# Left sums of the first layer kept unsplit and made by VectorE, with five weight stages and an earlier store of w_in's splits

## The chip, the cores and the metric

The kernel runs on one core of one Trainium2 chip. The metric is the device time of one execution in microseconds (us). Engines are named as the profile names them: PE (TensorE matmul), PEld (its weight loads), DVE (VectorE), ACT (ScalarE), POOL (GpSimd), SP (SyncE, which issues nearly all DMAs here).

## The reference

Three stages follow each other on 2304 tokens (4 batches of 576) of width 512.

```python
scores = scale * (q @ k.T)                     # 8 heads of 64
x = ((scores * Dmat) @ v)                      # Dmat: gamma ** (i - j), causal
h = x @ w_in;  x = relu(h) ** 2 @ w_out        # d_ff 2048
h = x @ w_in2; out = (h * clip(h + 3, 0, 6) / 6) @ w_out2
```

## The kernel before

Weights arrive as 64-bit floats and are decoded on the chip: for each piece of 128x512, `decode` gives four steps, two on ACT (`first`, L169 and L170, which read the staged words) and four instructions on DVE (`clamp` L173 and L176, `second` L182, `third` L188). A decoded fp32 tensor is then split into a high and a low fp32r part: ACT copies the high part, and the low part is a subtraction on DVE or POOL (`split_parts`, L192). Each matmul is done in three passes (high by high, high by low, low by high).

The first expert layer starts with a block of 768 tokens that runs over 16 chunks of 128 hidden units (`for c in range(NCH)`, L918). In chunk `c` PE does `h(c)` (24 matmuls, L428, in banks 6 and 7) and then `y(c-2)` (24 matmuls, L475). ACT takes `h` out of the banks (relu L444, square L447, high copy L448), so `h(c+1)` waits until the relus of chunk `c` have read them. DVE makes g's low parts (L451). Each chunk also decodes a piece A (w_out of the chunk before) and, up to chunk 13, a piece B (w_in for two chunks on), splits A (`wo`, low part on POOL) and B (`win`, low part on POOL), and stores the splits in HBM (`keep`, L406) for the blocks after it. Two `win` buffers alternate, and a staged weight is loaded into one of three buffers.

The remaining tokens run in five blocks of 768 (`BLOCKS`: two of the first layer, three of the second), 8 pairs of chunks each, with a Strassen scheme of seven products per pair (`pair`, L660; P1, P6, P2, P7, P5, P4, P3, each of 6 matmuls L675), between which the `y` steps of the pair before and side work are interleaved (`between(0)` to `between(6)`). The scheme needs four left operands per pair: w_in of two chunks (e = 0 and 1), and two sums of them, s0 and s1 (e = 2 and 3; P6 and P7 use e = 2, P5 and P3 use e = 3). `left_sums` (L500) makes the sums from decoded fp32 in four instructions of 128x256 on POOL. For the first layer this happens every second chunk, and `split_left` (L514) splits one of the two in each chunk (the tile `ready`: high on ACT, low on POOL), in chunks later than the sum; the split goes to HBM. `load_left` (L611) loads all four operands of pair k+1 from HBM at `between(0)` of pair k. The second layer's weights are decoded in time slots of seven per pair (`ready_slots`, 125 slots, in all pairs but the last of a block).

The order on each engine is that in which the code emits instructions; every engine's queue runs in order, SP's DMA issues too.

Of the kernel before, what the change touches and what calls it, by code (L numbers as in the profile page):

```python
# [74 lines left out]
def retention_moe_moe2(ctx, tc, qk, qk_last, kv, w_in, w_out, w_in2, w_out2, consts, out):  # L75

    nc = tc.nc
# [29 lines left out]
    turn = {"g": 0, "v": 0, "win": 0, "bounce": 0, "stage": 0, "decoded": 0}  # L107
# [388 lines left out]
    def store_late():  # L496
        while late_stores:
            keep(*late_stores.pop(0))

    def left_sums(a, b):  # L500
# [3 lines left out]
        op = nc.gpsimd.tensor_tensor  # L504
# [4 lines left out]
        return [a, b, s0, s1]  # L509
# [14 lines left out]
    def ready_slots():  # L524
# [16 lines left out]
        def sums(p):  # L541
            got["s", p] = left_sums(*(w32.pop((1, 2 * p + e, 0)) for e in range(2)))
# [68 lines left out]
    def load_left(k):  # L611
# [4 lines left out]
        for e in range(4):  # L616
            only = slice(1, 2) if e == 1 else slice(0, 2)
# [5 lines left out]
            lefts[j, p].append(t)  # L623

# [122 lines left out]
    halves = [(c, 0, c, 1) for c in range(1, NCH)]  # L747
# [6 lines left out]
    def next_load():  # L754

        turn["decoded"] += 1
        if coming and turn["decoded"] > 3:
            load_w(*coming.pop(0)[1:])

    with tc.manual_schedule():  # L760
# [152 lines left out]
        made = {}  # L913
# [4 lines left out]
        for c in range(NCH):  # L918
            mine, p = wins[c], c // 2
            h = emit_h(c)  # L920
            store_late()
            keep(("s", 0, p, c % 2), mine.rearrange("p a b n -> p (a b n)"), slice(c % 2, 2))
# [14 lines left out]
            for d in dec:  # L937
                for f in d:
                    f()
                next_load()  # L940
            if c >= 2:
                split_out(c - 1, nc.gpsimd)
            if c and c + 2 < NCH:
                split_in(c + 2)
            if c % 2:
                if c > 1:
                    split_left(0, p - 1, 3, made.pop(p - 1)[3])
                made[p] = left_sums(*(first_in[p][:, e] for e in range(2)))
            elif c:
                split_left(0, p - 1, 2, made[p - 1][2])  # L950
            while halves and halves[0][0] <= c:
                d = decode(*halves.pop(0)[1:])
                d.pop(0)()
                due.append(d)
# [11 lines left out]
        for d in due:  # L966
            for f in d:
                f()
            next_load()
        assert not halves  # L970
        split_out(NCH - 1, nc.gpsimd)
        pending = firsts(NCH - 2) + firsts(NCH - 1)
        store_late()
        for c in (NCH - 2, NCH - 1):
            keep(("o", 0, c), wouts[c].rearrange("p e n -> p (e n)"))
        highs[2]()
        lows[1]()
# [4 lines left out]
        lows[4]()  # L982
        load_left(1)
        uv = place("uv", [128, 4, HALF], F32, "u")
        us, vs = uv[:, :2], uv[:, 2:]
        rest = made.pop(NPAIR - 1)
        slots = [[] for _ in range(7)]
# [6 lines left out]
        for k in range(total):  # L994
# [91 lines left out]
```

## Time and profile before

| | |
|---|---|
| median of 3 runs | 875.61 us (875.46 to 879.59) |
| the profiled execution | 874.83 us |
| its span, first to last instruction | 873.0 us |
| busy: PE, PEld | 835.1 us (96%), 744.3 us |
| busy: DVE, ACT, POOL | 570.3, 457.6, 191.2 us |
| mean granted TensorE clock | 0.994 |

The span is the time between the first and the last instruction of the core; about 1.8 us of the execution lie outside it. Busy time is an average over stages; PE is busy 96% of the span, so 38 us of the span are left in which it does nothing.

### The profile page before, as it was taken

The numbers are of one execution on the slowest core, as the hardware profiler recorded it, in microseconds if no ns is written. First come the engines' busy times: TensorE is split into PE (matmuls) and PEld (weight loads), VectorE is DVE, ScalarE is ACT, GpSimd is POOL, SyncE is SP. The second block draws the span as 40 slices with busy tenths as digits, with TensorE's granted clock in tenths as the row PEclk, the third lists the DMA queues.
The fourth block names the chain that finished last, engine by engine and source line by source line (L and its number), as shares of the span: only waits on it lengthen the run. The fifth ranks groups of instructions, "written<-read, shape, count | busy, mean of one in ns | idle before, by whom it ended". The sixth has DMA issues, their size and how long they took to land.

```text
span 873.0 us, 14182 instructions
## 1 busy us (share of the span) xinstructions
PE 835.1 (96%) x5220; PEld 744.3 (85%) x5220; DVE 570.3 (65%) x954; ACT 457.6 (52%) x897; POOL 191.2 (22%) x170
## 2 busy tenths in 40 slices
PE   9989888888999999999999899999999999999997
PEld 7878777766899998899999798898898898899886
DVE  5878888888766776677666778546555446643534
ACT  1247666666756666756667654435433335433332
POOL 2354655657221330132121212100000000000000
PEclk9999999999899999999999999999999999999999
DMA  9994777797888989598987696946466453664532
GB/s 358 369 287 144 249 246 248 245 315 243 302 313 292 319 310 332 205 348 294 340 331 285 233 327 224 335 158 217 166 263 222 158 194 132 258 252 166 177 113 73
DMA packets 79115, 219.17 MB, mean 251 GB/s; under 512 B 8132, under 2 KB 24900, under 8 KB 79046
## 3 DMA queue, kind: packets, MB, share of 16 engines
q1 hardware_dynamic: 78466, 217.48, 70.8%
q8 instruction: 41, 0.67, 0.3%
q10 hardware_dynamic: 580, 0.79, 0.3%
q14 instruction: 28, 0.23, 0.1%
HBM read 167.38 MB, written 50.86 MB: 250 GB/s over the span
## 4 chain that ended last, share of the span: by engine, by line
PE 67%; DVE 13%; ACT 8%; DMA 7%; issue 3%; SPq 1%; POOL 1%; DVEq 0%; ACTq 0%; POOLq 0%
PE hps L675 30%; PE yps L635 20%; PE yps L475 10%; PE ytail L475 5%; DMA kvt<-in_kv_dram 3%; DMA stage<-in_w_in_dram 2%; DVE a L182 2%; DVE g L451 2%; DVE a L176 2%; ACT a L169 1%; ACT ready L194 1%; DVE wd L188 1%; DVE a L173 1%; DVE w L188 1%; ACT r L170 1%
## 5 line engine op out<-in xcount | busy, mean ns | idle before, releaser
L635 PE MATMUL yps<-wo,g 128*128 128x512 f32 x864 | 227.4, 394 | 3.6 <-DVE g L695 2.9
L675 PE MATMUL hps<-xlast,win 128*128 128x384 f32 x960 | 195.2, 338 | 1.3 <-DVE xlast L605 1.2
L635 PEld LDWEIGHTS yps<-wo,g 128*128 128x128 f32 x864 | 159.3, 188 | 29.2 <-DVE g L695 3.9
L675 PEld LDWEIGHTS hps<-xlast,win 128*128 128x128 f32 x960 | 167.7, 188 | 10.2 <-DVE xlast L605 1.5
L475 PE MATMUL yps<-g,wo 128*128 128x512 f32 x576 | 169.6, 400 | 3.1 <-ACT xop L600 1.4
L699 DVE TENSOR_TENSOR u<-hps,u 128x384 f32<-128x384 f32 x120 | 66.8, 557 | 159.7 <-PE hps L675 156.9
L675 PE MATMUL hps<-xop,win 128*128 128x384 f32 x720 | 147.9, 340 | 4.6 <-DVE xop L605 3.9
L675 PEld LDWEIGHTS hps<-xop,win 128*128 128x128 f32 x720 | 126.8, 190 | 12.0 <-DVE xop L605 4.3
L475 PEld LDWEIGHTS yps<-g,wo 128*128 128x128 f32 x576 | 102.0, 189 | 17.5 <-POOL wo L195 6.3
L475 PEld LDWEIGHTS ytail<-g,wo 128*128 128x128 f32 x576 | 94.4, 188 | 16.9
L693 ACT ACTIVATE g<-c 128x384 fp32r<-128x384 f32 x120 | 63.0, 525 | 84.3 <-DVE c L692 82.8
L475 PE MATMUL ytail<-g,wo 128*128 128x256 f32 x576 | 98.8, 280 | 0.0
L428 PE MATMUL hps<-xring,win 128*128 128x512 f32 (+1 forms) x384 | 72.4, 346 | 15.7 <-ACT r L444 15.7
L695 DVE TENSOR_TENSOR g<-c,g 128x384 fp32r<-128x384 f32 x120 | 70.7, 589 | 21.7 <-ACT g L693 21.4
L428 PEld LDWEIGHTS hps<-xring,win 128*128 128x128 f32 x384 | 61.1, 192 | 26.6 <-ACT r L444 18.0
L195 POOL TENSOR_TENSOR ready<-sums,ready 128x512 fp32r<-128x512 f32 x32 | 46.1, 1440 | 138.7 <-ACT ready L194 131.3
L718 ACT ACTIVATE c<-hps 128x384 f32<-128x384 f32 x40 | 19.7, 492 | 94.4 <-PE hps L675 94.4
L691 ACT ACTIVATE u<-c,three 128x384 f32<-128x384 f32 x72 | 44.4, 617 | 37.6 <-DVE c L699 36.4
L699 DVE TENSOR_TENSOR c<-hps,u 128x384 f32<-128x384 f32 x80 | 44.4, 555 | 24.4 <-PE hps L675 24.4
L182 DVE SCALAR_TENSOR_TENSOR a<-stage,a 128x512 int32<-128x512 int32 x64 | 52.1, 814 | 0.8
L692 DVE SCALAR_TENSOR_TENSOR c<-u,c 128x384 f32<-128x384 f32 x72 | 41.0, 570 | 13.4 <-ACT u L691 13.3
L173 DVE TENSOR_SCALAR a<-a 128x512 f32<-128x512 f32 x64 | 34.7, 543 | 21.3 <-ACT a L169 21.3
(95 smaller groups left out, 919.2 us busy)
## 6 DMA issues: line engine op xcount, KB each, us to landing
win<-kept SPq DMA_DIRECT2D x120, 512.0 KB
wo<-kept SPq DMA_DIRECT2D x80, 512.0 KB
kept<-ready SPq DMA_DIRECT2D x56, 512.0 KB
stage<-in_w_out_dram SPq DMA_DIRECT2D x32, 512.0 KB
win<-kept SPq DMA_DIRECT2D x40, 256.0 KB
kept<-wo SPq DMA_DIRECT2D x16, 512.0 KB
stage<-in_w_in_dram SPq DMA_DIRECT2D x16, 512.0 KB
qkt<-in_qk_dram SPq DMA_DIRECT2D x13, 512.0 KB
```

What stands on the lines that cost most here:

```text
L173: nc.vector.tensor_scalar(out=a, in0=a, scalar1=LEAST, scalar2=MOST, op0=ALU.max, op1=ALU.min)
L182: nc.vector.scalar_tensor_tensor(out=a.bitcast(I32), in0=high, scalar=-0x40000000, in1=a.bitcast(I32), op0=ALU.bitwise_and, op1=ALU.bitwis ...
L195: lambda: lo_engine.tensor_tensor(out=lo, in0=src, in1=hi.bitcast(F32), op=ALU.subtract),
L428: nc.tensor.matmul(out=h, lhsT=w[:, kk // 2, wp, kk % 2 * 128:][:, :128], rhs=xs[kk][xp][:, o:o + n], start=m == 0, stop=m == 3 * KD - 1,)
L475: nc.tensor.matmul(out=p, lhsT=w[:, wp, m * 128:m * 128 + 128], rhs=gt[:, gpart, o:o + n], start=first and e == 0 and not (k and m % 2), s ...
L635: nc.tensor.matmul(out=p, lhsT=gt[:, gpart, m * 128:m * 128 + 128], rhs=w[:, wp], start=first and e == 0, stop=last and e == 2,)
L675: nc.tensor.matmul(out=to, lhsT=wl[k][:, half if k != 1 else 0, wp, o], rhs=x[:, xp, f], start=first and m == 0, stop=last and m == 5, ski ...
L691: nc.scalar.activation(out=v, in_=c, func=ACTF.Relu, bias=three)
L692: nc.vector.scalar_tensor_tensor(out=c, in0=v, scalar=6.0, in1=c, op0=ALU.min, op1=ALU.mult)
L693: nc.scalar.activation(out=hi, in_=c, func=ACTF.Copy)
L695: lambda: nc.vector.tensor_tensor(out=lo, in0=c, in1=hi.bitcast(F32), op=ALU.subtract)
L699: nc.vector.tensor_tensor(out=out_, in0=to, in1=x, op=ALU.add)
```

## The change

It has five parts.

1. In the chunk loop the first layer's left sums are made by DVE instead of POOL, and stored as they are (fp32, one store of 512 KB per pair, key `f`) instead of as two splits (two stores of 512 KB, key `s`). The 16 `ready` splits of the first layer (ACT and POOL) go from the loop and its end.
2. For pairs of the first layer `load_left` loads the two sums unsplit (256 KB each instead of 512), and new steps `parts_of_left` split them: for pair k+1, the high part of e = 2 on ACT at `between(4)` of pair k, its low part on DVE at `between(5)`, and e = 3 one step later. For pair 0 all this is in chunk 15.
3. Five staging buffers instead of three while the first layer's weights are loaded (two more loads in chunks 2 and 3, two fewer when the second layer's loads begin).
4. The split of w_in for chunk c+1 is stored in chunk c behind the sums' store, before the store of w_out's split; the last two w_out splits are made in chunk 15 with the low part on DVE. w_out of chunk 15 is decoded together with that of chunk 14.
5. In each chunk the ACT steps of decode A come before the split of `win` and no longer after it. The second layer's slots begin seven slots sooner, as the first layer's last `split_left` steps go.

```diff
-        if turn["stage"] <= 3:
-            t = place(f"t{2 + turn['stage']}", [128, DM], mybir.dt.int64, "stage")
+        tags = ("t3", "t4", "t5") if turn["stage"] <= 3 else ("t3", "t4", None, None, None)
+        tag = None if l else tags[(turn["stage"] - 1) % len(tags) if turn["stage"] <= 3 else (turn["stage"] - 2) % 5]
...
-    def left_sums(a, b):
+    def left_sums(a, b, engine):
...
-        op = nc.gpsimd.tensor_tensor
+        op = engine.tensor_tensor
...
+            if l == 0 and e > 1:
+                t = place(f"w{4 * (k % 2) + e}", [128, 2, 2, 256], F32R, "win")
+                nc.sync.dma_start(
+                    out=t[:, 1].rearrange("p a n -> p (a n)").bitcast(F32),
+                    in_=kept["f", 0, p][:, 512 * (e - 2):512 * (e - 1)],
+                )
+                lefts[j, p].append(t.rearrange("p b a n -> p a b n"))
+                continue
...
+    def parts_of_left(k, e):
+
+        hi, lo = (lefts[divmod(k, NPAIR)][e][:, :, wp] for wp in range(2))
+        return split_parts(hi, lo, lo.bitcast(F32), nc.vector)
...
-    halves = [(c, 0, c, 1) for c in range(1, NCH)]
+    halves = [(min(c, NCH - 2), 0, c, 1) for c in range(1, NCH)]
...
-            store_late()
-            keep(("s", 0, p, c % 2), mine.rearrange("p a b n -> p (a b n)"), slice(c % 2, 2))
...
+            if c in (2, 3):
+                load()
+            store_late()
+            for n, w in ((c, mine), (c + 1, wins.get(c + 1))):
+                if w is not None and (n != c or not c):
+                    keep(("s", 0, n // 2, n % 2), w.rearrange("p a b n -> p (a b n)"), slice(n % 2, 2))
             if c >= 2:
-                split_out(c - 1, nc.gpsimd)
+                split_out(c - 1, nc.gpsimd if c < NCH - 1 else nc.vector)
+            if c == NCH - 1:
+                split_out(c, nc.vector)
+            while halves and halves[0][0] <= c:
+                due.append(decode(*halves.pop(0)[1:]))
+            for d in due[:1]:
+                d.pop(0)()
             if c and c + 2 < NCH:
                 split_in(c + 2)
             if c % 2:
-                if c > 1:
-                    split_left(0, p - 1, 3, made.pop(p - 1)[3])
-                made[p] = left_sums(*(first_in[p][:, e] for e in range(2)))
-            elif c:
-                split_left(0, p - 1, 2, made[p - 1][2])
-            while halves and halves[0][0] <= c:
-                d = decode(*halves.pop(0)[1:])
+                whole = left_sums(*(first_in[p][:, e] for e in range(2)), nc.vector)[1]
+                late_stores.append((("f", 0, p), whole.rearrange("p a n -> p (a n)")))
+            for d in due[1:]:
                 d.pop(0)()
...
+            if c == NCH - 1:
+                for e in (2, 3):
+                    parts_of_left(0, e)[0]()
+                lows[1]()
+                for e in (2, 3):
+                    parts_of_left(0, e)[1]()
...
-        slots[2].append(lambda: split_left(0, NPAIR - 1, 2, rest[2]))
-        slots[5].append(lambda: split_left(0, NPAIR - 1, 3, rest[3]))
-        slots += ready_slots()
+        slots = ready_slots()
...
+            if k + 1 < total and BLOCKS[(k + 1) // NPAIR][0] == 0:
+                for i, e in ((4, 2), (5, 3)):
+                    for n in range(2):
+                        side[i + n].append(lambda e=e, n=n: parts_of_left(k + 1, e)[n]())
```

ACT's queue in chunk 3, from the split of w_out on. `wo`, `win` and `ready` are split tiles, `a<-stage` and `r<-stage` the first steps of a decode, `r<-hps` the relu of the next chunk. Before:

```order
L194 ACTIVATE wo<-wd 128x512
L194 ACTIVATE win<-w_1334 128x2x256
L194 ACTIVATE ready<-sums 128x2x256
L169 ACTIVATE a<-stage 128x512
L170 ACTIVATE r<-stage 128x512
L169 ACTIVATE a<-stage 128x512
L170 ACTIVATE r<-stage 128x512
L444 ACTIVATE r<-hps 128x512
```

And now:

```order
L196 ACTIVATE wo<-wd 128x512
L171 ACTIVATE a<-stage 128x512
L172 ACTIVATE r<-stage 128x512
L196 ACTIVATE win<-w_1327 128x2x256
L171 ACTIVATE a<-stage 128x512
L172 ACTIVATE r<-stage 128x512
L446 ACTIVATE r<-hps 128x512
```

Decode A's steps have moved ahead of `win`, and `ready` is gone.

DVE's queue at the turn from an odd chunk to the next: the last two steps of decode B (`w_` is its output), and the first steps of decode A of the next chunk. Before:

```order
L182 SCALAR_TENSOR_TENSOR a<-stage,a 128x512
L188 ISA w_1150<-a,r 128x1024
L173 TENSOR_SCALAR a<-a 128x512
L176 TENSOR_SCALAR a<-a 128x512
L182 SCALAR_TENSOR_TENSOR a<-stage,a 128x512
L188 ISA wd<-a,r 128x1024
```

And now:

```order
L184 SCALAR_TENSOR_TENSOR a<-stage,a 128x512
L190 ISA w_1142<-a,r 128x1024
L507 TENSOR_TENSOR sums<-w_1015 128x256
L508 TENSOR_TENSOR sums<-sums,w_1015 128x256
L509 TENSOR_TENSOR sums<-w_1015 128x256
L510 TENSOR_TENSOR sums<-w_1015,sums 128x256
L175 TENSOR_SCALAR a<-a 128x512
L178 TENSOR_SCALAR a<-a 128x512
L184 SCALAR_TENSOR_TENSOR a<-stage,a 128x512
L190 ISA wd<-a,r 128x1024
```

Four instructions stand between the two decodes.

DVE's queue at the turn from chunk 15 to pair 0. `xop` and `xlast` are low parts of right operands (`lows`), `xall` a sum of operands, `u<-hps` the first use of P6's result. Before, from the last decode on:

```order
L173 TENSOR_SCALAR a<-a 128x512
L176 TENSOR_SCALAR a<-a 128x512
L182 SCALAR_TENSOR_TENSOR a<-stage,a 128x512
L188 ISA wd<-a,r 128x1024
L605 TENSOR_TENSOR xop<-t,xop 128x384 x2
L605 TENSOR_TENSOR xop<-xall,xop 128x384 x2
L605 TENSOR_TENSOR xlast<-xall,xlast 128x384 x2
L605 TENSOR_TENSOR xlast<-t,xlast 128x384 x2
L583 TENSOR_TENSOR xall<-xall,t 128x384 x2
L699 TENSOR_TENSOR u<-hps,u 128x384
```

And now:

```order
L190 ISA wd<-a,r 128x1024
L197 TENSOR_TENSOR wo<-wd,wo 128x512 x2
L507 TENSOR_TENSOR sums<-w_2119 128x256
L508 TENSOR_TENSOR sums<-sums,w_2119 128x256
L509 TENSOR_TENSOR sums<-w_2119 128x256
L510 TENSOR_TENSOR sums<-w_2119,sums 128x256
L607 TENSOR_TENSOR xop<-t,xop 128x384 x2
L197 TENSOR_TENSOR win<-win 128x512 x2
L607 TENSOR_TENSOR xop<-xall,xop 128x384 x2
L607 TENSOR_TENSOR xlast<-xall,xlast 128x384 x2
L607 TENSOR_TENSOR xlast<-t,xlast 128x384 x2
L585 TENSOR_TENSOR xall<-xall,t 128x384 x2
```

The lows of the last two w_out splits, the last sums and the lows of pair 0's left operands have come into this queue.

## Rows read from the trace of the kernel before

**Rows 1.** Busy time by stretch: us, PE, PEld, VectorE, ScalarE, GpSimd (instructions), clock, DMA, GB/s

```profile
...
80.27:88.68 8.41, 8.41 (x50) 7.32 (x49) 6.44 (x9) 4.51 (x10) 4.52 (x4) 1.00 0.57 176
...
109.22:129.76 20.54, 17.80 (x97) 14.69 (x97) 16.34 (x21) 13.54 (x27) 12.56 (x10) 1.00 0.75 243
...
211.29:234.86 23.57, 18.99 (x92) 16.64 (x91) 19.04 (x31) 15.62 (x33) 10.29 (x9) 0.86 0.82 288
234.86:480.00 245.14, 243.04 (x1377) 224.85 (x1376) 166.37 (x290) 158.09 (x315) 52.10 (x49) 1.00 0.84 305
480.00:548.00 68.00, 62.99 (x314) 54.80 (x313) 54.88 (x94) 36.02 (x69) 13.68 (x14) 1.00 0.73 258
...
```

**Rows 2.** Waits in chunks 4 to 15: us in total, times, longest

```profile
...
ACT win L194 <- DVE w L188: 32.0, 10, 4.4
...
PE hps L428 <- ACT r L444: 14.3, 10, 3.2
...
```

**Rows 3.** The chain through chunks 8 and 9: start us, us, what

```profile
...
132.32 3.85 DMA stage<-in_w_in_dram
...
145.66 0.70 DVE w L188
...
146.97 0.62 ACT ready L194
...
149.81 0.49 ACT r L444
...
```

**Rows 4.** Timeline of chunks 4 to 6: start us, us, engine, line, instruction

```profile
...
96.06 1.48 POOL L195 TENSOR_TENSOR ready<-sums,ready 128x512 fp32r<-128x512 f32 x1
...
96.42 1.41 DVE L176 TENSOR_SCALAR a<-a 128x512 int32<-128x512 int32 x1
...
109.87 0.69 DVE L188 CUSTOM_DVE_ANT_0 wd<-a,r 128x1024 uint16<-128x1024 uint16 x1
...
110.48 0.42 DVE L173 TENSOR_SCALAR a<-a 128x512 f32<-128x512 f32 x1
...
110.93 0.43 DVE L176 TENSOR_SCALAR a<-a 128x512 int32<-128x512 int32 x1
...
111.28 1.02 DVE L451 TENSOR_TENSOR g<-r,g 128x512 fp32r<-128x512 f32 x2
...
112.21 0.68 DVE L182 SCALAR_TENSOR_TENSOR a<-stage,a 128x512 int32<-128x512 int32 x1
...
```

**Rows 5.** Groups of instructions in chunks 4 to 15

```profile
...
L195 POOL TENSOR_TENSOR wo<-wd,wo 128x512 fp32r<-128x512 f32 x12 | 19.6, 1630 | 21.3 <-ACT wo L194 21.3
...
L195 POOL TENSOR_TENSOR win<-w,win 128x512 fp32r<-128x512 f32 x11 | 14.4, 1306 | 24.0 <-ACT win L194 18.6 <-PE ytail L475 4.1 <-PE hps L428 1.3
...
L451 DVE TENSOR_TENSOR g<-r,g 128x256 fp32r<-128x256 f32 x12 | 5.5, 462 | 0.0
...
```

**Rows 6.** Timeline, last chunks and first Strassen pairs; idle time and its releaser in brackets

```profile
...
192.74 6.06 PE L428 MATMUL hps<-xring,win 128*128 128x512 f32 x24 [3.25 <-ACT r L444]
...
218.88 2.01 PE L675 MATMUL hps<-xop,win 128*128 128x384 f32 x5 [3.90 <-DVE xop L605]
...
246.29 0.52 ACT L693 ACTIVATE g<-u 128x384 fp32r<-128x384 f32 x1
...
250.72 1.21 PE L675 MATMUL hps<-xop,win 128*128 128x384 f32 x6
...
284.17 0.73 PE L475 MATMUL yps<-g,wo 128*128 128x512 f32 x2 [0.33 <-DVE g L695]
...
```

**Rows 7.** Groups of instructions of VectorE in the first layer's pairs

```profile
...
L699 DVE TENSOR_TENSOR u<-hps,u 128x384 f32<-128x384 f32 x46 | 25.6, 557 | 45.0 <-PE hps L675 42.6 <-ACT ready L194 1.3 <-issue 0.6
...
L195 DVE TENSOR_TENSOR ready<-wd,ready 128x512 fp32r<-128x512 f32 x11 | 7.6, 690 | 14.0 <-ACT ready L194 14.0
...
```

**Rows 8.** Timeline of SyncE's DMA issues in pair 4

```profile
...
285.22 3.72 SPq L619 DMA_DIRECT2D win<-kept  x4
```

**Rows 9.** The chain through chunk 13: start us, us, what

```profile
...
182.57 6.81 DMA stage<-in_w_in_dram
...
```

More of the change, by code (lines that the diff above doesn't have):

```diff
@@ L105, in retention_moe_moe2 @@
     xall = const.tile([128, KD, NT], F32, name="xall")
-    turn = {"g": 0, "v": 0, "win": 0, "bounce": 0, "stage": 0, "decoded": 0}
+    turn = {"g": 0, "v": 0, "win": 0, "bounce": 0, "stage": 0, "decoded": 0, "fewer": 2}
     def place(tag, shape, dtype, name):
@@ L131, in load_w @@
         turn["stage"] += 1
-        if turn["stage"] <= 3:
-            t = place(f"t{2 + turn['stage']}", [128, DM], mybir.dt.int64, "stage")
+        tags = ("t3", "t4", "t5") if turn["stage"] <= 3 else ("t3", "t4", None, None, None)
+        tag = None if l else tags[(turn["stage"] - 1) % len(tags) if turn["stage"] <= 3 else (turn["stage"] - 2) % 5]
+        if tag:
+            t = place(tag, [128, DM], mybir.dt.int64, "stage")
         else:
@@ L494, in retention_moe_moe2, with store_late @@
     late_stores = []
-    def store_late():
-        while late_stores:
+    def store_late(keeping=0):
+        while len(late_stores) > keeping:
             keep(*late_stores.pop(0))
-    def left_sums(a, b):
+    def left_sums(a, b, engine):
         both = place("t5", [128, 2, 512], F32, "sums")
@@ L508, in left_sums @@
         op(out=half(s1, 1), in0=half(a, 1), in1=half(s0, 0), op=ALU.subtract)
-        return [a, b, s0, s1]
+        return [a, b, s0, s1], both
     def bounce():
@@ L541, in sums @@
         def sums(p):
-            got["s", p] = left_sums(*(w32.pop((1, 2 * p + e, 0)) for e in range(2)))
+            got["s", p] = left_sums(*(w32.pop((1, 2 * p + e, 0)) for e in range(2)), nc.gpsimd)[0]
         def out_split(c):
@@ L756, in next_load @@
         turn["decoded"] += 1
-        if coming and turn["decoded"] > 3:
+        if coming and coming[0][1] and turn["fewer"]:
+            turn["fewer"] -= 1
+        elif coming and turn["decoded"] > 3:
             load_w(*coming.pop(0)[1:])
@@ L912, in retention_moe_moe2 @@
         ywork = y_first(0, {})
-        made = {}
         def firsts(c):
@@ L945, in retention_moe_moe2 @@
             if c % 2:
-                if c > 1:
-                    split_left(0, p - 1, 3, made.pop(p - 1)[3])
-                made[p] = left_sums(*(first_in[p][:, e] for e in range(2)))
-            elif c:
-                split_left(0, p - 1, 2, made[p - 1][2])
-            while halves and halves[0][0] <= c:
-                d = decode(*halves.pop(0)[1:])
+                whole = left_sums(*(first_in[p][:, e] for e in range(2)), nc.vector)[1]
+                late_stores.append((("f", 0, p), whole.rearrange("p a n -> p (a n)")))
+            for d in due[1:]:
                 d.pop(0)()
-                due.append(d)
             if c >= LAG:
@@ L965, in retention_moe_moe2 @@
                 (highs[0], lows[0], highs[1])[c - NCH + 3]()
[L966 to L971, printed above, removed]
+            if c == NCH - 1:
[4 more added lines that the diff above has]
+                    parts_of_left(0, e)[1]()
+        assert not halves and not due
         pending = firsts(NCH - 2) + firsts(NCH - 1)
-        store_late()
-        for c in (NCH - 2, NCH - 1):
-            keep(("o", 0, c), wouts[c].rearrange("p e n -> p (e n)"))
         highs[2]()
-        lows[1]()
         highs[3]()
@@ L982, in retention_moe_moe2 @@
         lows[4]()
+        store_late()
+        for c in (NCH - 2, NCH - 1):
+            keep(("o", 0, c), wouts[c].rearrange("p e n -> p (e n)"))
         load_left(1)
@@ L985, in retention_moe_moe2 @@
         us, vs = uv[:, :2], uv[:, 2:]
-        rest = made.pop(NPAIR - 1)
-        slots = [[] for _ in range(7)]
-        slots[2].append(lambda: split_left(0, NPAIR - 1, 2, rest[2]))
-        slots[5].append(lambda: split_left(0, NPAIR - 1, 3, rest[3]))
-        slots += ready_slots()
+        slots = ready_slots()
         flip = False
```

## The prediction

> **What bounds the kernel now.** I read the busy times by stretch first. In the two blocks of the first layer and in the second layer PE hardly rests: it is busy 243.04 of 245.14 us from pair 1 to 480 us, and 62.99 of 68.00 us at the start of the second layer [rows 1]. The idle time lies in the chunk loop and at its end. Chunk 3 takes 8.41 us with PE busy throughout, which is the floor of a chunk; from chunk 4 on two chunks take 20.54 us, in which PE is busy 17.80, DVE 16.34, ACT 13.54 and POOL 12.56 [rows 1]. No engine is full, so a loop of waits must set the time.
>
> The waits say which. PE waits ten times, 14.3 us, for ACT's relu (L444), which gives back the bank of h; ACT in turn waits ten times, 32.0 us, for DVE's last decode step before it splits `win` [rows 2]. The chain shows the loop: DVE's `third` of decode B at 145.66, then ACT's `ready` at 146.97 and four decode steps, and only at 149.81 the relu that lets PE go on [rows 3]. DVE itself then waits for the decode steps queued behind `win` and `ready`. A second loop shows in the even chunk: the load of w_in, 3.85 us, ends on the chain at 136.17 [rows 3], since three staging buffers let a load start only when the decode just before has freed one.
>
> DVE's share of that loop is stretched. Its `clamp` step L176 takes 0.43 us at 110.93, while POOL is idle, but 1.41 us at 96.42, beside POOL's 1.48 us `ready` split [rows 4]. Alone, four decodes of 0.42 + 0.43 + 0.68 + 0.69 us and two pairs of g lows of 1.02 us make 10.9 us for two chunks [rows 4], so 16.34 - 10.9 = 5.4 us are stretch beside 12.56 us of POOL, 0.43 us for each us of POOL.
>
> **Chunk loop, chunks 4 to 15.** They run from 88.68 to 211.29 [rows 1], 122.6 us, six pairs of chunks. The change takes `ready` and the sums from POOL and leaves one `wo` and one `win` low per chunk, 1.63 + 1.31 us [rows 5], 5.9 us in two chunks. DVE gains four sums of 128x256; the nearest row is g's low of that shape, 0.46 us [rows 5], so 1.85 us. DVE then has 10.9 + 1.85 + 0.43 x 5.9 = 15.3 us in two chunks. ACT loses two `ready` copies and has about 12.3 us. Both are under PE's floor of 2 x 8.41 = 16.82 us. The order matters more than these sums: decode A's ACT steps now stand ahead of `win`, so DVE goes from decode B, or from the sums, straight into decode A, and the relu no longer stands behind a DVE result of the same chunk that is late. After a chunk's second low DVE has decode B left (1.4 us, at worst beside the 1.6 us of POOL's `wo`), so `win`, two ACT decode steps and the relu fit before the bank is needed, with some 4 us to spare. A load has five buffers, over two chunks of lead, against 3.85 us of landing, and the second loop goes too. DMA moves one store of 512 KB less in two chunks: 243 GB/s x 20.54 us = 5.0 MB become 4.5 MB, 262 GB/s in 17.1 us, and 305 GB/s are moved later [rows 1]. I take 17.1 us for two chunks: the floor and 0.3 us for single waits. That is 6 x 17.1 = 102.6 us, a gain of **20.0 us**. Bounds: the floor itself (gain 21.7); and DVE held for all of POOL's time, 10.9 + 1.85 + 5.9 = 18.7 us for two chunks (gain 10.4).
>
> The last bound can be weighed. L176 at 96.42 ends at 97.83, just behind POOL's end at 97.54 [rows 4]: that instruction was held whole, though over the loop only 0.43 of POOL's time came back as stretch. The Trainium skill's page "SBUF — State Buffer", section "Who interferes with whom", has VectorE and GpSimd share a port pair under an exclusive lock, where the later instruction is blocked wholly. The trace agrees on the single instruction. By this rule alone the sums on DVE, with two inputs, would be held too and the pair would take up to the 18.7 us above; by the loop's mean it takes 15.3 us of DVE. I go by the mean, since DVE also rests while it waits for ACT.
>
> **From the loop to pair 1.** Pair 0 takes 23.57 us [rows 1]; a pair that waits for nothing takes 250.72 - 234.86 = 15.86 us [rows 1, 6], so 7.7 us are lost: 3.90 us before P6 behind DVE's low of its operand [rows 6], and the rest in smaller waits and where PE runs slower. The granted clock of this stretch is 0.86, between its levels of 2.4 and 1.2 GHz [rows 1]; a group of 24 matmuls after a wait of 3.25 us took 6.06 us [rows 6]. Now P6 needs more from DVE: after h(15) ends, ACT's passes and the last low (about 2 us), decode steps of 1.4 us, two `wo` lows of 0.69 [rows 7], four sums 1.85, a pair of `xop` lows of 1.1 (two of the 0.557 us size [rows 7]), and the first `win` low 0.69: 8.4 us. PE has y(13), P1 and a y step to do, half a chunk of 8.41 us and two of the 15 steps that make a pair of 15.86 us, 6.3 us in all: a wait of 2.1 us. Then P7 waits for the use of P6's result, which stands behind one `win` low and four pairs of 1.1 us, 5.7 us with itself, against 4.2 us of PE work: 1.5 us. The second layer's slots now begin here too (two decodes, 4.4 us of DVE), and I give pair 1's first y 1.1 us of waiting. In all 4.7 us instead of 7.7, none of the single waits as long as the 3.25 us behind which the clock fell: a gain of **3.0 us**. Bounds: all 7.7 us go; or all that decode time comes on top, a loss of 4.4.
>
> **First layer's pairs.** Each of 15 pairs, 0 to 14, gets two lows on DVE, 0.69 us each [rows 7], and two high copies on ACT. DVE has room: in pairs 1 to 15 it rests 245.14 - 166.37 = 78.8 us, 45.0 of it before the u adds alone [rows 1, 7]. But the place counts: the low of e = 2 stands at `between(5)`, ahead of the add of P3 and of g's c21 low, which the next pair's first y step needs. That step was 0.33 us late in pair 4 where a slot's work also stood there [rows 6], so the 0.69 us come on top in such pairs. I take **+2.5 us**: 0.7 in three heavy pairs, and 0.4 for the pairs with operand splits. Bounds: nothing, or 0.69 us in 14 pairs, 9.7. Without the DVE rest the cover would be gone, and two lows in 16 pairs would cost 22 us.
>
> **Start of the second layer.** PE loses 68.00 - 62.99 = 5.0 us there, with DVE busy 54.88 [rows 1]. As the slots begin seven sooner, one pair fewer is loaded with decodes: **-1.0 us**, between -5.0 and +1.0.
>
> **The sum.** Against the profiled execution: 874.83 - 20.0 - 3.0 + 2.5 - 1.0 = 853.3 us. The median of the runs is 0.8 us over that execution, so I predict **854 us**. The bounds all taken together give 840 and 880.
>
> **Rivals.** *DVE is held for all of POOL's time* and sets the chunk loop at 18.7 us for two chunks. For: the held L176. Against: the mean of 0.43. Worked out: 9.6 us more, 863.6 us. The same time would come from DMA slowing: 4.5 MB at the old 243 GB/s take 18.5 us. *The pairs take it back*: every e = 2 low lands on the path, 9.7 instead of 2.5 us, 861 us. For: the 0.33 us wait, and POOL still sums the second layer's weights beside it. Against: DVE's rest. *A better case*: the turn and the second layer's start lose all their waits, 845 us or less; DVE's longer queue at the turn speaks against it. *Slower than before*: ACT reaches the new high copy about 12 us into a pair (the copy before it ends at 246.81 in the pair that starts at 234.86) [rows 6]; if the load of e = 2 lands later than that, ACT, and behind it act(c21) and then g and y, wait. One late case is in sight: issues at 285.22 that take 3.72 us [rows 8], and the longest landing on the chain is 6.81 us [rows 9]; together 295.8, 13.4 us into the pair that started three pairs after 234.86, at 282.4. Past some 13 us each us costs up to 15 us over 15 pairs, so it turns the result at about 14.5 us; at 15 us it costs 30 us, 884 us. Against: that pair is the exception, and the sums' loads are halved. *The change does nothing*: a load or store that bounds the loop anyway, 874 us; but the relu's wait has a DVE result on the chain each time.
>
> **Chances.** The forecast, 845 to 859: 0.66. Below 845: 0.06. DVE held or DMA slow, 859 to 867: 0.12. Pairs take it back: 0.08. Nothing: 0.04. Slower: 0.04. The range of 845 to 867 us leaves out 0.14; the forecast's own is 848 to 859. A change of 0.5%, 4.4 us, is about what can be told from none here; so faster 0.92, same 0.04, slower 0.04.
>
> **What the profile would show.** Right: two chunks in 16.8 to 17.4 us; no PE wait for the relu; ACT's wait for DVE's `third` down to a few us; POOL busy near 6 us and DVE near 15 us in two chunks; L176 mostly near 0.43 us; P6 of pair 0 waiting about 2 us. Wrong: PE still waiting for the relu with DVE full; ACT waiting for a `win` load inside the pairs; y steps waiting for g lows in most pairs; a granted clock under 0.9 at the turn.

## The result, and the profile after

The changed kernel takes 852.23 us (median of 4 runs, 850.68 to 855.8) against 875.54 us in the same session: a ratio of 0.9738 (95% interval 0.9697 to 0.9778). The profiled execution is one of 850.68 us with a span of 848.9 us; the prediction was 854.

Busy time by stretch: one early chunk, two chunks of the loop, pairs 0 and 1, the first layer's later pairs, the start of the second layer (columns as in [rows 1]).

```profile
80.45:88.83 8.38, 8.38 (x50) 7.36 (x49) 8.07 (x13) 6.04 (x13) 2.87 (x2) 1.00 0.88 297
105.59:122.35 16.76, 16.76 (x98) 14.73 (x97) 16.12 (x25) 12.70 (x25) 6.22 (x4) 1.00 0.83 268
189.39:211.09 21.70, 18.32 (x92) 16.00 (x91) 20.71 (x42) 16.31 (x34) 0.00 (x0) 0.92 0.62 227
211.09:227.67 16.58, 16.39 (x92) 14.73 (x91) 13.67 (x22) 12.14 (x24) 6.43 (x6) 1.00 0.87 303
227.67:455.00 227.33, 222.54 (x1260) 205.71 (x1259) 172.20 (x297) 158.28 (x316) 52.29 (x47) 1.00 0.79 281
455.00:525.00 70.00, 67.44 (x343) 59.57 (x342) 52.62 (x92) 37.61 (x74) 11.31 (x11) 1.00 0.73 260
```

Two chunks take 16.76 us and PE is busy in all of it: PE is now the bound of the loop, with DVE close behind (16.12 us). In [rows 1] two chunks took 20.54 us with no engine full.

Starts of h and of the pairs' P1 and P6 in the two timelines cut the gain up. Each row is a time between the same two instructions of before and after; the six add up to the spans' difference, 24.1 us. The +2.5 was forecast for pairs 0 to 14 and stands in the row of pairs 2 to 15.

| stretch | before | after | change | predicted |
|---|---|---|---|---|
| start to h(4) | 88.68 | 88.83 | +0.15 | 0 |
| chunks 4 to 15 | 122.61 | 100.56 | -22.05 | -20.0 |
| pairs 0 and 1 | 39.43 | 38.28 | -1.15 | -3.0 |
| pairs 2 to 15 | 225.06 | 227.65 | +2.59 | +2.5 |
| pair 16 to P6 of pair 20 | 71.75 | 68.71 | -3.04 | -1.0 |
| the rest | 325.47 | 324.87 | -0.60 | 0 |

Waits in chunks 4 to 15 of the changed kernel (columns as in [rows 2]; PE has no row among them):

```profile
POOL wo L197 <- ACT wo L196: 38.9, 11, 4.3
POOL win L197 <- ACT win L196: 21.1, 11, 2.4
ACT win L196 <- issue: 14.4, 6, 2.5
ACT win L196 <- POOL wo L197: 4.8, 4, 1.2
ACT win L196 <- DVE w L190: 1.2, 1, 1.2
```

ACT's 32.0 us behind DVE's third step [rows 2] are down to 1.2, and PE's wait for the relu is gone. The wait of DVE that closed the loop has no row any more either; before it was

```profile
DVE a L173 <- ACT a L169: 18.0, 11, 1.9
```

What waits now is POOL, and nothing waits long for it (ACT 1.2 us at most). For ACT's 14.4 us marked "issue" the profile shows no releaser.

Groups of instructions there (line, engine, operation, tiles, count | busy us, mean ns | idle):

```profile
L184 DVE SCALAR_TENSOR_TENSOR a<-stage,a 128x512 int32<-128x512 int32 x23 | 20.3, 881 | 0.4
L453 DVE TENSOR_TENSOR g<-r,g 128x256 fp32r<-128x256 f32 x12 | 11.7, 972 | 0.0
L190 DVE CUSTOM_DVE_ANT_0 w<-a,r 128x1024 uint16<-128x1024 uint16 x11 | 12.5, 1137 | 0.4
L178 DVE TENSOR_SCALAR a<-a 128x512 int32<-128x512 int32 x23 | 9.8, 428 | 0.8
L510 DVE TENSOR_TENSOR sums<-w,sums 128x256 f32<-128x256 f32 x6 | 9.1, 1523 | 0.0
L509 DVE TENSOR_TENSOR sums<-w 128x256 f32<-128x256 f32 x6 | 2.5, 418 | 0.0
```

The sums do what one expects of 128x256 (0.42 us) except the last, L510, which is held in all six pairs. The timeline shows by what:

```profile
109.29 0.42 DVE L509 TENSOR_TENSOR sums<-w 128x256 f32<-128x256 f32 x1
109.37 1.50 POOL L197 TENSOR_TENSOR win<-w,win 128x512 fp32r<-128x512 f32 x1 [1.34 <-ACT win L196]
109.63 1.53 DVE L510 TENSOR_TENSOR sums<-w,sums 128x256 f32<-128x256 f32 x1
```

L509 has begun before POOL and isn't lengthened; L510 begins behind POOL and ends 0.29 us after POOL does. L178, 1.41 us at one place of [rows 4], is never held now (428 ns in the mean): what is held is decided by what DVE has next when POOL starts, and the list above shows the load moved to L184, L190 of decode B, L453 and L510.

PE's waits from pair 0 on, to the start of pair 20:

```profile
192.40 0.50 PE L477 MATMUL yps<-g,wo 128*128 128x512 f32 x1 [1.33 <-DVE wo L197]
193.80 0.45 PE L690 MATMUL hps<-xop,win 128*128 128x384 f32 x1 [0.55 <-ACT win L196]
195.11 0.44 PE L690 MATMUL hps<-xop,win 128*128 128x384 f32 x1 [0.86 <-DVE xop L607]
196.18 1.65 PE L690 MATMUL hps<-xop,win 128*128 128x384 f32 x4 [0.63 <-DVE win L197]
...
246.33 0.73 PE L477 MATMUL yps<-g,wo 128*128 128x512 f32 x2 [1.39 <-DVE g L710]
...
490.97 0.73 PE L650 MATMUL yps<-wo,g 128*128 128x512 f32 x2 [1.54 <-DVE g L710]
507.77 0.74 PE L650 MATMUL yps<-wo,g 128*128 128x512 f32 x2 [0.70 <-DVE g L710]
```

The one wait of 3.90 us before P6 [rows 6] has become three of 0.55, 0.86 and 0.63, with a new one of 1.33 ahead of them.

### The profile page after: what moved, and what is told of

Read it like the earlier page. It is cut to its first block, busy times and chain, and to the rows that moved or that the text cites. A ratio compares the mean times of both kernels' runs of the same rounds, so it can differ in the third digit from the quotient of the medians.

```text
span 848.9 us, 14161 instructions
## 1 busy us (share of the span) xinstructions
PE 826.9 (97%) x5220; PEld 742.1 (87%) x5220; DVE 586.5 (69%) x1020; ACT 465.8 (55%) x913; POOL 137.7 (16%) x120
## 4 chain that ended last, share of the span: by engine, by line
PE 73%; DVE 12%; DMA 7%; ACT 5%; issue 2%; SPq 1%; POOL 0%; DVEq 0%; ACTq 0%; POOLq 0%
PE hps L690 29%; PE yps L650 22%; PE yps L477 10%; PE ytail L477 5%; PE hps L430 4%; DMA kvt<-in_kv_dram 4%; DVE a L184 2%; DVE wd L190 1%; DVE g L710 1%; DVE g L453 1%; DVE u L714 1%; DVE a L175 1%; DVE a L178 1%; DMA wo<-kept 1%; DVE c L714 1%
## 5 line engine op out<-in xcount | busy, mean ns | idle before, releaser
L477 PE MATMUL yps<-g,wo 128*128 128x512 f32 x576 | 167.1, 398 | 3.9 <-DVE g L710 1.4
L430 PE MATMUL hps<-xring,win 128*128 128x512 f32 (+1 forms) x384 | 69.6, 337 | 1.2 <-ACT r L446 1.2
L184 DVE SCALAR_TENSOR_TENSOR a<-stage,a 128x512 int32<-128x512 int32 x64 | 57.1, 893 | 0.8
L171 ACT ACTIVATE a<-stage 128x512 f32<-128x512 f32 x64 | 42.4, 662 | 5.3 <-DMA stage<-in_w_in_dram 5.3
L172 ACT ACTIVATE r<-stage 128x512 int32<-128x512 uint32 x64 | 42.3, 661 | 0.0
```

Of the source, the lines that this page charges most:

```text
L171: nc.scalar.activation(out=a, in_=high.bitcast(F32), func=ACTF.Abs)
L172: nc.scalar.activation(out=r, in_=low.bitcast(U32), func=ACTF.Copy, scale=2.0 ** -29)
L184: nc.vector.scalar_tensor_tensor(out=a.bitcast(I32), in0=high, scalar=-0x40000000, in1=a.bitcast(I32), op0=ALU.bitwise_and, op1=ALU.bitwis ...
L430: nc.tensor.matmul(out=h, lhsT=w[:, kk // 2, wp, kk % 2 * 128:][:, :128], rhs=xs[kk][xp][:, o:o + n], start=m == 0, stop=m == 3 * KD - 1,)
L477: nc.tensor.matmul(out=p, lhsT=w[:, wp, m * 128:m * 128 + 128], rhs=gt[:, gpart, o:o + n], start=first and e == 0 and not (k and m % 2), s ...
```

## The experiments

Each time is a median with the runs' extremes; the ratio is to the kernel before, run beside it on the same chip (873.9 to 875.6 us). "Changed" is the changed kernel.

**1. The changed kernel again**, beside runs 8 to 10, without an edit.

> The changed kernel once more, as the reference of the three runs beside it: 850 to 854 us, the chunk loop at 16.8 us for two chunks.

852.06 us (850.63 to 853.2), ratio 0.974 [0.9721, 0.9759]. Its profile also shows how much one profile leaves uncertain. In the opening h(2) waits 1.81 us for a relu, against 1.16 in the first profile, and the matmuls behind that run slower (6.03 us for 24 that otherwise take 4.34). Pairs 0 and 1 take 36.84 us in place of 38.28, with the wait for `wo` gone. In the profiles of the changed kernel and its variants, run 6 aside, that wait at h(2) is 0.2 to 2.8 us. So one profile settles the turn to about 1.5 us, not better.

**2. The order undone.** ACT's steps of decode A behind the split of `win` again:

```diff
-            for d in due[:1]:
-                d.pop(0)()
             if c and c + 2 < NCH:
                 split_in(c + 2)
+            for d in due[:1]:
+                d.pop(0)()
```

> The changed kernel, but in each chunk ACT's two steps of decode A stand behind the split of win again. DVE is busy 16.1 of 16.76 us in two chunks of the changed kernel, so it has 0.6 us to lose. If the order on ACT closes the loop, DVE rests twice in two chunks while win and two decode steps run (about 1.2 to 1.8 us each, as it did before), so two chunks take 18.5 to 19.7 us and the kernel 862 to 870 us. If only POOL's lighter load counts, or the buffers, two chunks stay at 16.8 us and the kernel at about 852 us.

857.74 us (856.64 to 859.37), ratio 0.9801 [0.9783, 0.9819]; the order is worth 5.5 us on top of the rest, about half of the least that was expected (10 us). Two chunks:

```profile
124.50:142.30 17.80, 17.34 (x98) 14.76 (x97) 15.69 (x25) 12.49 (x25) 5.70 (x4) 1.00 0.73 247
```

**3. The order alone**, in the kernel before:

```diff
+            while halves and halves[0][0] <= c:
+                due.append(decode(*halves.pop(0)[1:]))
+            for d in due[:1]:
+                d.pop(0)()
             if c and c + 2 < NCH:
                 split_in(c + 2)
...
-            while halves and halves[0][0] <= c:
-                d = decode(*halves.pop(0)[1:])
+            for d in due[1:]:
                 d.pop(0)()
-                due.append(d)
```

> The kernel before with one edit: ACT's two steps of decode A stand ahead of the split of win. If the order closes the loop, DVE's rests go: two chunks take 17 to 18.5 us instead of 20.5, and the kernel 855 to 864 us. If DVE's stretch by POOL or the three buffers set the loop, little changes: 870 us or more.

869.1 us (866.54 to 871.48), ratio 0.9929 [0.9903, 0.9954], which lies between the two expectations. Chunks 6 and 7, and waits in chunks 4 to 13:

```profile
107.23:126.23 19.00, 17.40 (x96) 14.77 (x96) 18.39 (x21) 13.56 (x27) 12.59 (x11) 1.00 0.81 263
```

```profile
ACT win L194 <- DVE w L188: 17.0, 8, 3.6
...
PE hps L428 <- ACT r L444: 7.4, 3, 3.9
...
ACT a L169 <- DMA stage<-in_w_in_dram: 4.4, 3, 2.7
```

ACT's wait for DVE's third step (32.0 us in chunks 4 to 15 before) and PE's for the relu (14.3) are about halved, but DVE, better fed, is now nearly full: the same instructions that took 16.34 us of 20.54 in [rows 1] take 18.39 of 19.00 beside the same POOL work. From chunk 10 to 13 the gain is lost again: the four chunks take 42.1 us, before 42.4. There loads of `w_in` into the three staging buffers land late; two of 5.51 and 7.84 us stand on the chain ahead of ACT's decode step and the relu. Over chunks 4 to 15 the order alone gains 6.2 us. Whether five buffers would have kept the rest wasn't run.

**4. The sums on POOL** (unsplit, with the new order):

```diff
-                whole = left_sums(*(first_in[p][:, e] for e in range(2)), nc.vector)[1]
+                whole = left_sums(*(first_in[p][:, e] for e in range(2)), nc.gpsimd)[1]
```

> The changed kernel with the left sums of the chunk loop made by POOL, still unsplit. POOL then has some 10.2 us in two chunks instead of 6.2; DVE loses 2.8 us of its own but is held more. If DVE's stretch goes with POOL's time at 0.43 to 0.57 us for each us, DVE has 15.3 to 16.7 us and the loop stays at its floor: 850 to 854 us. If the move to DVE is what frees the loop, the old sums would bring two chunks to 18 us or more: 859 us or more.

854.42 us (853.62 to 855.78), ratio 0.9763 [0.9745, 0.9781].

```profile
106.85:123.61 16.76, 16.76 (x99) 14.73 (x98) 16.15 (x20) 12.27 (x25) 9.89 (x8) 1.00 0.76 262
```

The loop is at the floor here too up to chunk 11; chunks 12 to 15 take 35.47 us in place of 33.52. In the steady chunks DVE's busy time is the same with 20 instructions in place of 25 (16.15 against 16.12 us): what it gets as work when the sums are moved to it, it saves as time held.

**5. Unsplit sums alone**: edits 2 and 4 together.

> The changed kernel with the old order of ScalarE's decode steps and with the left sums on GpSimd: what is left in the chunk loop is that the sums are not split, the five weight buffers and the earlier store. With the old order and the sums on VectorE two chunks took 17.8 us, with the new order and the sums on GpSimd 16.76. Theory, that dropping the splits of the sums does most and the engine of the sums next to nothing: 17.6 to 18.3 us for two chunks, about 858 us. Rival, that the move of the sums to VectorE pays where the order is old: 19 us or more for two chunks, from 865 us.

863.67 us (861.47 to 865.04), ratio 0.9851 [0.9822, 0.9881].

```profile
126.64:145.58 18.94, 17.36 (x96) 14.75 (x97) 15.60 (x21) 12.49 (x25) 9.69 (x8) 1.00 0.69 235
```

Neither expectation is met fully; it lies close to the rival. With the old order the move of the sums to DVE is worth 18.94 - 17.80 = 1.1 us for two chunks (5.5 us over chunks 4 to 15), with the new order nothing in the steady chunks, where PE's floor hides it, and 2.0 us in chunks 12 to 15.

**6. Three staging buffers:**

```diff
...
-        tags = ("t3", "t4", "t5") if turn["stage"] <= 3 else ("t3", "t4", None, None, None)
-        tag = None if l else tags[(turn["stage"] - 1) % len(tags) if turn["stage"] <= 3 else (turn["stage"] - 2) % 5]
+        tag = f"t{2 + turn['stage']}" if turn["stage"] <= 3 else None
...
-            if c in (2, 3):
-                load()
```

> The changed kernel with three staging buffers as before. If a late load was a limit of its own, ACT's decode steps wait for loads in most chunks again and two chunks take 17.5 to 19 us: 857 to 866 us. If the order and POOL's load are enough, a load still has over half a chunk of lead against some 4 us of landing, and the time stays within 3 us of 852.

857.16 us (855.25 to 858.77), ratio 0.9795 [0.977, 0.982]. From chunk 3 on two chunks take 16.8 us; what is lost goes in chunk 2:

```profile
ACT win L195 <- DMA kept<-win: 6.4, 1, 6.4
...
PE hps L429 <- ACT r L445: 6.0, 1, 6.0
```

ACT's split of `win` has to wait until the store of the split before it has read the buffer, and that store is issued at 70.89, behind four loads of w_in on SP, the first of which goes out only at 68.75, some 8 us after the load before it. In the changed kernel this wait of ACT is 1.5 us (2.1 in run 1). So in the changed kernel the five buffers carry the opening, not the steady loop.

**7. The store at its old place**, behind each chunk's h, five buffers kept:

```diff
             h = emit_h(c)
+            store_late()
+            keep(("s", 0, p, c % 2), mine.rearrange("p a b n -> p (a b n)"), slice(c % 2, 2))
...
-            store_late()
-            for n, w in ((c, mine), (c + 1, wins.get(c + 1))):
-                if w is not None and (n != c or not c):
-                    keep(("s", 0, n // 2, n % 2), w.rearrange("p a b n -> p (a b n)"), slice(n % 2, 2))
```

> The changed kernel with the stores of w_in's splits and of the sums back at the place they had before, each issued right behind the matmuls of its own chunk. Theory, that the earlier store only makes room in the queue: two chunks stay at 16.8 us and the time within 2 us of 852. Rival, that the store gives back the buffer of the split which ScalarE needs two chunks on: ScalarE's first step of the win split then waits for the store, some 2 us in a chunk, and two chunks take 17.5 us or more, from 856 us.

852.43 us (851.81 to 855.27), ratio 0.9732 [0.9703, 0.976]: the earlier store brings nothing that can be told from no change. The loop stays at 16.76 us up to chunk 11; chunks 12 to 15 take 34.43 us in place of 33.52:

```profile
105.42:122.18 16.76, 16.76 (x99) 14.73 (x98) 16.11 (x25) 12.68 (x25) 6.21 (x4) 1.00 0.82 269
```

**8. The slots seven later again:**

```diff
-        slots = ready_slots()
+        slots = [[] for _ in range(7)] + ready_slots()
```

> The changed kernel with the second layer's slots beginning seven slots later, in pair 1 as before. If the earlier slots are what shortened the start of the second layer (by 3.2 us, from pair 16 to pair 20), those 3 us come back, and pairs 0 and 1 lose some 1 to 2 us of waits: 1 to 3 us slower than the changed kernel. If the start of the second layer gained from something else, it stays, and the kernel is equal or 1 to 2 us faster.

853.6 us (853.01 to 853.9), ratio 0.9756 [0.974, 0.9773]. Pair 16 to P6 of pair 20 takes 71.73 us, before's 71.75, against 68.69 in run 1, and before's waits are back. The time is 1.5 us above run 1's, as the first expectation has it; pairs 0 and 1, at 38.07 us, gained nothing by it.

```profile
469.36 1.14 PE L690 MATMUL hps<-xlast,win 128*128 128x384 f32 x5 [1.20 <-DVE xlast L607]
...
509.45 0.72 PE L650 MATMUL yps<-wo,g 128*128 128x512 f32 x2 [1.55 <-DVE g L710]
526.24 0.72 PE L650 MATMUL yps<-wo,g 128*128 128x512 f32 x2 [0.69 <-DVE g L710]
```

**9. The left lows later**: e = 2 at `between(5)` and `(6)`, e = 3 at `between(1)` and `(2)` of the pair that uses it.

```diff
...
-                for i, e in ((4, 2), (5, 3)):
-                    for n in range(2):
-                        side[i + n].append(lambda e=e, n=n: parts_of_left(k + 1, e)[n]())
+                for n in range(2):
+                    side[5 + n].append(lambda n=n: parts_of_left(k + 1, 2)[n]())
+            if l == 0:
+                for n, f in enumerate(parts_of_left(k, 3)):
+                    side[1 + n].append(f)
```

> The changed kernel with the new splits at other places: for e = 2 the high part at between(5) and the low part at between(6), behind g's c21 low; for e = 3 in the pair that uses it, at between(1) and between(2), where DVE rests before the adds. The same number of instructions. If the place costs the 2.6 us by which pairs 2 to 15 became longer, 1.5 to 3 us of it go (849 to 851 us); also pair 0 needs one split less before P6 (0.7 us). If it is DVE's and ACT's greater load as such, the time stays within 1 us of the changed kernel.

852.53 us (851.42 to 854.2), ratio 0.9747 [0.9727, 0.9766]. Pairs 2 to 15 take 226.50 us against 227.58 in run 1, so the place costs 1.1 us of the 2.6. In the profiled execution the gain is given back elsewhere: P1 of pair 0 starts 2.07 us later (the wait at h(2), which the edit doesn't touch, is 2.77 us here), and from 490 us on the granted clock reads 0.72 behind a wait of 1.56 us, where run 1 has 1.00 behind one of 1.55:

```profile
490.00:496.00 6.00, 4.34 (x12) 3.67 (x13) 5.34 (x10) 3.22 (x7) 3.58 (x5) 0.72 0.93 351
```

**10. The turn too**: run 9, with the last `wo` low and the last sums behind the operands of P6 (and pair 1's `load_left` behind the sums).

```diff
...
-            if c == NCH - 1:
-                split_out(c, nc.vector)
...
-            if c % 2:
+            if c % 2 and c < NCH - 1:
...
         highs[2]()
         lows[2]()
+        split_out(NCH - 1, nc.vector)
...
+            if k == 0:
+                side[1] += [lambda: sums_of_pair(NPAIR - 1), lambda: load_left(1)]
```

> The kernel with the splits later, and at the turn from chunk 15 to pair 0 the low part of the last w_out split and the last four sums moved behind the operands of P6 (the sums to between(1) of pair 0). If DVE's queue before P6 sets the loss there, the waits of P6 (0.55, 0.86 and 0.63 us) go to under 0.7 us in all, the granted clock stays up, and it is 2 to 4 us faster than with the splits alone. If the queue is as long in another place, the waits move to P7 and the y steps, and it gains under 1 us.

850.86 us (849.0 to 852.21), ratio 0.9724 [0.9705, 0.9744], not to be told from run 1, nor, by the intervals, from run 9. P6 waits 0.33 us instead of 2.05, but other waits take its place, and pairs 0 and 1 take 37.16 us, no less than run 1's 36.84:

```profile
194.84 0.50 PE L477 MATMUL yps<-g,wo 128*128 128x512 f32 x1 [1.38 <-DVE wo L197]
196.38 0.97 PE L690 MATMUL hps<-xop,win 128*128 128x384 f32 x4 [0.33 <-DVE win L197]
201.20 1.32 PE L690 MATMUL hps<-xlast,win 128*128 128x384 f32 x6 [0.70 <-DVE u L714]
205.00 0.98 PE L690 MATMUL hps<-xlast,win 128*128 128x384 f32 x4 [1.07 <-DVE win L197]
```

DVE is busy 20.71 of 21.70 us in pair 0 of the changed kernel with POOL at rest, and 19.84 of 20.36 here, so by these figures it is DVE's sum of work that counts there more than its order.

**11. All lows on DVE**, so that POOL rests in the steady loop:

```diff
-        split_to(w[:, :, 0], w[:, :, 1], w32[0, c, 0].rearrange("p (a n) -> p a n", a=2), nc.gpsimd)
+        split_to(w[:, :, 0], w[:, :, 1], w32[0, c, 0].rearrange("p (a n) -> p a n", a=2), nc.vector if c > 4 else nc.gpsimd)
...
-                split_out(c - 1, nc.gpsimd if c < NCH - 1 else nc.vector)
+                split_out(c - 1, nc.gpsimd if c < 4 else nc.vector)
```

> The changed kernel with GpSimd's lows of wo (from chunk 4) and of win (from chunk 5) made by VectorE, so that GpSimd does nothing in the steady chunk loop. Theory, that VectorE's time beyond its work alone comes from GpSimd: VectorE 10.9 + 1.7 + 4 x 0.69 = 15.3 us in two chunks with no instruction longer than it is alone, against 16.1 now; two chunks stay at PE's 16.76 us, 851 to 853 us. Rival, that the stretch has another source (the DMA or ScalarE): it stays, VectorE has 16.1 + 2.8 = 18.9 us and sets two chunks at that, 865 us.

849.01 us (847.22 to 852.52), ratio 0.9695 [0.9657, 0.9734]. Two chunks, and groups of DVE in eight of them:

```profile
140.33:157.09 16.76, 16.76 (x99) 14.73 (x97) 14.57 (x29) 12.75 (x25) 0.00 (x0) 1.00 0.80 267
```

```profile
L184 DVE SCALAR_TENSOR_TENSOR a<-stage,a 128x512 int32<-128x512 int32 x17 | 11.7, 688 | 0.3
L190 DVE CUSTOM_DVE_ANT_0 w<-a,r 128x1024 uint16<-128x1024 uint16 x9 | 6.2, 692 | 0.3
L197 DVE TENSOR_TENSOR wo<-wd,wo 128x512 fp32r<-128x512 f32 x9 | 6.2, 684 | 0.0
L453 DVE TENSOR_TENSOR g<-r,g 128x256 fp32r<-128x256 f32 x8 | 3.4, 423 | 1.1 <-ACT g L450 1.0
L510 DVE TENSOR_TENSOR sums<-w,sums 128x256 f32<-128x256 f32 x4 | 1.7, 418 | 0.0
```

With four instructions more DVE is busy 1.55 us less. L184 is back from 881 to 688 ns, L190 of decode B from 1137 to 692, L453 from 972 to 423, L510 from 1523 to 418: the stretch of the steady chunks came from POOL, and the rival falls. The gain itself lies at the turn: pairs 0 and 1 take 34.92 us against 36.84 to 38.28, and the granted clock of pair 0 is 1.00. In pair 0 DVE is busy 17.95 us, 1.3 less than in run 1 (19.25); that this is work done earlier, in the loop, is likely but not shown.

**12. Runs 10 and 11 together.**

> The lows of w_out and w_in on VectorE in the chunk loop (as in the run with GpSimd idle there) together with the later places of the left lows, the last sums and the last wo low (as in the run with the turn changed). If the two gains add, the time is some 1 us under the first alone, 847.5 to 848.5 us, with the chunk loop at 16.76 us for two chunks and pair 0 shorter by 1 us; if both remove the same waits at the turn, it stays at 849.

848.55 us (845.29 to 850.62), ratio 0.9703 [0.968, 0.9726]: no gain over run 11 that the runs can tell. Pairs 0 and 1 take 34.12 us, 0.8 less; the two edits mostly remove the same waits. These two are the fastest kernels here; run 11's upper end is 0.9734 and run 1's lower end 0.9721, so by the intervals alone the two are not apart.

## Why the prediction was right, and where it was not

**The mechanism of the chunk loop held.** That no engine was full and a chain of relu, `win` split and third step set the time is borne out: the three waits named went away together and the loop fell to PE's floor. The term was -20.0 and is -22.05. I had added 0.3 us for two chunks above the floor, and there is nothing above it; the floor itself is 8.38, not 8.41 us, which is why the gain lies just past the bound of 21.7. That the whole sum came out within 2 us of the median has a part of luck: the loop gained 2.05 us more than forecast and the second layer's start 2.04 more, the turn 1.85 less.

**The second loop, the late loads**, was not one of its own in the changed kernel: with three buffers in place of five its chunks 4 to 15 take the same 100.6 us (run 6). It did show in run 3, with three buffers, the splits still there and only the order new, from chunk 10 on.

**"The order matters more than these sums" did not hold as it was put.** Two steady chunks in us, from the runs above, and behind them chunks 4 to 15 as a whole:

| | old order | new order |
|---|---|---|
| sums split, on POOL | 20.54; 122.6 (before) | 18.9 to 19.0; 116.4 (run 3) |
| sums unsplit, on POOL | 18.94; 111.5 (run 5) | 16.76; 102.5 (run 4) |
| sums unsplit, on DVE | 17.80; 106.0 (run 2) | 16.76; 100.6 (changed) |

In two steady chunks the order alone brings 1.5 us, leaving out the splits alone 1.6, and the move of the sums 1.1 as long as the order is old. Over all twelve the order alone brings 6.2 us, leaving out the splits 11.1. The lower two rows also have the five buffers and the earlier store, which by runs 6 and 7 bring nothing in the steady loop of the changed kernel; what they bring with the old order wasn't run. No single part reaches the floor. The order and the missing splits together do in the steady chunks, and the move of the sums then brings only 2.0 us, in chunks 12 to 15. The split of `ready` is what I under-weighted: besides 1.48 us of POOL it took 0.62 us of ACT ahead of the relu [rows 3, 4].

**The time of DVE was under-sized.** I forecast 15.3 us for two chunks; 16.12 were measured, the balance of two errors. Run 11 gives DVE's own work without POOL: 14.57 us with four lows of 0.69, so 14.57 - 2.76 = 11.8 us for the changed kernel, where I had put 10.9 + 1.85 = 12.75. Its 6.22 us of POOL cost 16.12 - 11.8 = 4.3 us, 0.69 for each us, not 0.43. Single instructions give the same: in chunks 6 and 7 each of the four POOL lows lengthens one DVE instruction, L190 from 0.69 to 1.67 us, L510 from 0.42 to 1.53, L453 from 0.42 to 1.52 and L184 from 0.69 to 1.80, 4.3 us in all.

By the same reckoning (11.8 less four sums of 0.42, 10.1 us) the kernel before lost 6.2 us to 12.56 of POOL, 0.50, and run 3, with the same work and DVE nearly full, 8.3 us to 12.59, 0.66. Where DVE rests while POOL works, POOL's time costs little. The `win` low of before, then of the changed kernel:

```profile
94.80 1.30 POOL L195 TENSOR_TENSOR win<-w,win 128x512 fp32r<-128x512 f32 x1 [1.29 <-ACT win L194]
95.84 0.54 DVE L173 TENSOR_SCALAR a<-a 128x512 f32<-128x512 f32 x1 [1.78 <-ACT a L169]
```

```profile
118.50 1.29 POOL L197 TENSOR_TENSOR win<-w,win 128x512 fp32r<-128x512 f32 x1 [2.41 <-ACT win L196]
118.53 1.80 DVE L184 SCALAR_TENSOR_TENSOR a<-stage,a 128x512 int32<-128x512 int32 x1
```

Before, DVE rested through most of it and lost 0.12 us (L173 takes 0.42 alone); now it loses 1.11. So "I go by the mean, since DVE also rests" was the weak step: the change took that rest away. DVE's rest as a share does not give the price, though: in run 2 DVE rests 2.1 of 17.80 us and still loses 0.68 for each us of POOL, in run 4 it rests 0.6 of 16.76 and loses 0.61. What counts first is whether POOL's time falls on the rest. The error did no harm here, as 16.12 still fits under 16.76; the spare time was 0.6 us, not the 1.8 between 15.3 and the 17.1 that I gave the loop.

**DVE held for all of POOL's time**, the rival with 18.7 us for two chunks, did not come. The mechanism is real, the price is not: an instruction in flight when POOL starts goes on, the one behind it is held (109.37 above) and ends 0.3 to 0.6 us after POOL, less than its own time. So of POOL's 6.22 us DVE lost 4.3. The Trainium skill's page "SBUF — State Buffer", section "Who interferes with whom", says of VectorE's modes that use two ports that whoever issues first has the shared pair for its whole instruction, and that VectorE instructions with two inputs contend with GpSimd's reads; the trace agrees in L510, 1523 ns beside POOL and 418 without it, and the sum over the loop costs less than POOL's whole time, as just said.

**From the loop to pair 1** I gave 3.0 us; 1.15 were gained in the first profile and 2.6 (39.43 - 36.84) in that of run 1. P6's wait was forecast at 2.1 us and is 0.55 + 0.86 + 0.63 = 2.04, which is close partly by luck, as the first of the three is a wait for ACT and my account was of DVE's queue. P7's 1.5 and y's 1.1 us didn't come. What I missed is that the granted clock could still fall, 0.92 over pair 0, though no single wait reached 3.25 us, as I had written: four matmuls of P6 behind these waits took 1.65 us, in run 10 they took 0.97. And a wait of 1.33 us for the last `wo` low, now on DVE, is new in this profile and missing in run 1's.

**The first layer's pairs** came out in sum as put, +2.59 for +2.5, but not by the account that I gave. PE waits in four pairs, 1.39, 0.97, 1.20 and 1.23 us, the third of them for a load of `wo` and the last for ACT; before it waited in three, 0.33, 1.35 and 0.27. Run 9 shows that the place of the lows is 1.1 us of it, less than the three heavy pairs alone in my account (2.1). What makes up the other 1.5 us stays open. The earlier slots don't: with them undone (run 8) pairs 2 to 15 take 227.41 us, against 227.58 in run 1.

**The start of the second layer** had the right cause and a third of the size: -3.04 for -1.0. Run 8 takes the earlier slots away and the whole gain with them (71.73 against before's 71.75). Seven slots are a pair's whole load of decode. In run 8, as before, PE waits four times from the end of pair 16 to the start of pair 17, 1.20 + 0.38 + 0.65 + 0.42 = 2.65 us; in the changed kernel none of the four is there, and the two waits of 1.54 and 0.70 further on only come a pair sooner. Those 2.65 us are what I valued at 1.0.

**The rivals.** The pairs taking it back, and the change doing nothing, are refuted by the table of stretches; the better case of 845 us was not reached. Slower than before, by a late load of e = 2, didn't come either: from 189 to 455 us no wait of ACT for the load of a left operand shows. Nor did the loop run into DMA: 268 GB/s were moved in it.

## What to carry to other kernels

A rate at which one engine slows another, read from a kernel in which the slowed engine rests meanwhile, can be too low for the kernel in which that rest is gone; read it from an instruction alone and beside the other, or from a stretch in which the engine is full. When work leaves a chain of waits between queues, ask for each part alone whether it closes the loop: here neither the order nor the missing splits did, both together brought the steady chunks to PE's floor, and the move of the sums that came with them was needed for the last four chunks alone. And once a loop is at its floor, lighter work on an engine can still pay at the turn to the next stage, as in run 11, where that engine was the one nearly full.

## What was not expected of the hardware

- More instructions on VectorE in less time: 29 in 14.57 us with GpSimd at rest, 25 in 16.12 us beside 6.22 us of GpSimd. The four GpSimd lows of two chunks, 6.22 us, cost VectorE 4.3 us; made by VectorE itself they take 2.76.
- The granted clock fell, over parts of stretches, from 2.4 towards 1.2 GHz behind waits far under 3.25 us: its mean was 0.92 over pair 0 behind 1.33, 0.55, 0.86 and 0.63 us, 0.92 again in run 1 without the first of these, and 0.72 in run 9 from 490 us on behind one of 1.56 us. In run 10 it stayed at 1.00 behind 1.38, 0.33, 0.70 and 1.07 us, and in run 1 behind 1.55. What decides between these isn't settled.
